# A three-layer fused kernel: the gate's 64-channel chunk in three passes, late weight chunks' low parts on VectorE, six slots' tap sums on TensorE, and a new order

## The chip, the cores and the metric

The kernel runs on one core of one Trainium2 chip. The metric is device microseconds of one execution; of several executions the median is given. The engines are TensorE (PE), VectorE (DVE), ScalarE (ACT), GpSimd (POOL) and SyncE (SP), which here issues every DMA.

## What is computed

Two sequences of 4160 tokens with 192 channels go through three layers, one after another.

```python
# 1: windowed attention, 8 heads, 7 taps
w = exp(weight_gen - max); w = w / (sum(w) + 1e-9)          # over the 7 taps
x = einsum('bshk,bskhg->bshg', w, the last 7 rows of x)
# 2: token-shift mix and a gated square-relu layer, 192 -> 1024 -> 192
xk = mu_k * x + (1 - mu_k) * x_prev                         # x_prev: the row before
xr = mu_r * x + (1 - mu_r) * x_prev
x = sigmoid(xr @ w_r) * (relu(xk @ w_k) ** 2 @ w_v)
# 3: 192 -> 1024 -> 192 with a 3-tap convolution along the sequence
h = relu(x @ w_in)
out = (h * sigmoid(conv3(h, conv_w))) @ w_out
```

The weights arrive in float64, x, weight_gen, `mu_k` and `mu_r` in float32, and the result is float32.

## The kernel before

**Tiles.** The 4160 tokens of a sequence are cut into ten tiles `i`: two of 238 tokens, seven of 476 and one of 352 (`SIZES`). Each is done for both sequences `b`. A partition of the attention stage holds 2, 4 or 3 neighbouring tokens, its slots `l`. The 192 channels are cut into 128 and 64, the 1024 hidden channels into eight chunks `fi`.

**Precision.** A float32 product is made of fp32r passes: a value is split into a high part, which fp32r holds, and a low part, what is left. An ACT cast makes the high part, and a subtract on DVE or POOL the low part. A product against the 192 input channels takes 5 matmul passes (`passes_in`: three of 128 channels, and two in which the 64 remaining channels' high and low inputs lie in the two halves of one 128-lane tile, `xB`). A product from a hidden chunk back to 192 channels takes 5 as well (`out_passes`): `W[:, fi, 2]` has the high part of the 64 remaining output channels in its lower and the low part in its upper 64 columns, and the two halves of the result are added at the end.

**Weights.** Sixteen chunks of weights (`prepare`) are loaded one after another; `narrow` turns float64 bits into float32 in a PSUM bank: an ACT `Prelu`, a shift, a mask and a multiply on DVE, then an identity matmul and a sign matmul on PE. `split` then casts the high part on ACT, subtracts it by a sign matmul on PE, and copies the low part out on ACT. The bank `py` of `narrow` is `pc0`, which later is one of the two banks of the third layer.

**Attention.** For each slot, `token` makes one product of 1344 elements a partition (7 taps x 192) on POOL and then three adds (576, 384 and 192 elements) that sum the taps. In tile 0 alone seven identity matmuls on PE make the sum, and ACT copies it out. The DMA of a tile's rows (`attention.load`) goes into one of two buffers. `softmax` prepares the tap weights; for tiles 3 to 9 its steps run in between, tile by tile.

**Mixing and the layers.** `mixing` transposes tokens to channels on PE, mixes them with the row before (DVE), and splits them, the low parts on POOL; the 64-channel parts go to `xB` by DMA. `gate_r` makes the two chunks of r, `moe1` the eight hidden chunks, `mix_out` multiplies by r and writes the split result to `x2_b`, whose rows 0 and 1 are the 128 channels' high and low part, row 2 the 64 channels' high part (in both halves), and row 3 their high part again in lanes 0 to 63 and their low part in lanes 64 to 127. `moe2` reads it, its fifth pass row 3, and does convolution, sigmoid and `w_out`; `store` adds the two halves and sends the result out.

**Order.** Nothing is issued in the order of the code. Each step is put in a plan at a time (`at`), which the table `ORDER` shifts for single entries by their running number; the plan, in order of time, gives each operation a priority, and `schedule` then issues them by a list schedule with a cost of its own for each kind (`cost`). What comes out is a fixed order on each engine. SP issues DMAs in that order, and a DMA that waits holds all behind it. Line 237, in `schedule`, issues every operation, so all rows of the profile bear it and operations are told apart by their tiles: `pa`, `pc`, `am`, `ar`, `bm` and `br` are PSUM banks (`pa` first products and transposes, `am` and `ar` the second product of layer two, `pc` and `bm`, `br` those of layer three), `prod` and `tok` belong to attention, `xA`, `xB`, `rm` and `mk` to mixing, `s` and `g` are split hidden chunks. `stage` holds weights early on, and softmax sums, `q` and mixing's buffers later.

Of the kernel before, what the change touches and what calls it, by code (L numbers as in the profile page):

```python
# [30 lines left out]
LAG = 12  # L31

# [4 lines left out]
ALONE = 7  # L37
# [55 lines left out]
def f(ap):  # L93
    return ap.bitcast(F32)


class Program:
# [40 lines left out]
    def cost(self, eng, method, out, ins, pointer):  # L138
# [3 lines left out]
        if method == "dma_start":  # L142
            return 0.45, 0.0
# [108 lines left out]
def conv_moe_kernel(ctx: ExitStack, tc: tile.TileContext, xp, wg_first, wg_rest, mus, w_k, w_v, w_r, w_in, conv_w, w_out, out):  # L252
# [35 lines left out]
    mu = new("mu", [128, 4])  # L288
# [22 lines left out]
    wz_r = Ring([t.rearrange("p a b -> p (a b)") for t in g_r.tiles[:2]])  # L311
    rows_r = ring("rows", 2, [128, max(SLOTS) + PAD, DM])
# [16 lines left out]
    sw = new("sw", [128, sum(slots), KS, NH])  # L329
# [67 lines left out]
    on_pe = [False]  # L397

    def narrow(st, n):
# [5 lines left out]
        if on_pe[0]:  # L405

            zr = wz_r()[:, :n]
            ACT.activation(px, f(hi), ACTF.Prelu, scale=2.0 ** -112, alpha=-(2.0 ** 32))
            DVE.tensor_scalar(z, x, 3, None, op0=ALU.logical_shift_left)
            DVE.tensor_scalar(y, z, 0xFF800000, None, op0=ALU.bitwise_and)  # L410
            DVE.scalar_tensor_tensor(out=zr, in0=lo, scalar=2.0 ** -52, in1=py, op0=ALU.mult, op1=ALU.mult)
            PE.matmul(px, lhsT=ident, rhs=f(z), start=True, stop=False, skip_group_check=True)
            PE.matmul(px, lhsT=signs[:, 0:128], rhs=zr, start=False, stop=True, skip_group_check=True)
            return px
        ACT.activation(px, f(hi), ACTF.Copy, scale=2.0 ** -112)
        DVE.tensor_scalar(x, x, 3, None, op0=ALU.logical_shift_left)
        DVE.scalar_tensor_tensor(out=x, in0=hi, scalar=0x80000000, in1=x, op0=ALU.bitwise_and, op1=ALU.bitwise_or)
        DVE.tensor_scalar(y, x, 0xFF800000, None, op0=ALU.bitwise_and)
        DVE.scalar_tensor_tensor(out=f(z), in0=lo, scalar=2.0 ** -52, in1=py, op0=ALU.mult, op1=ALU.mult)
# [58 lines left out]
    def prepare(first, seq):  # L478

        for j, (t, (load, n, go)) in enumerate(seq):  # L480
# [5 lines left out]
            def use(st=st, n=n, go=go, j=j):  # L486
                on_pe[0] = j < 16
                go(narrow(st[0], n))
# [595 lines left out]
```

## Time and profile before

| | |
|---|---|
| median of 3 runs | 736.1 us (734.06, 736.1, 736.75) |
| the profiled execution's own time | 739.15 us |
| its span | 737.3 us |
| mean granted clock of PE | 0.989 of full speed |
| busy: PE, DVE, ACT, POOL | 706.5, 580.1, 646.6, 537.8 us |
| the same, share of the span | 96%, 79%, 88%, 73% |
| share of PE in the chain that ended last | 80%; POOL 8%, ACT 6%, DVE 2%, DMA 1% |

The busy times are averages over very different stages: until some 120 us the weights are prepared and the first, half-size tiles run; then comes a steady stretch; POOL has its attention work until about 515 us and little after that; from 720 us on the last chunks run out. Rows of matmuls overlap, so a row's length is not its price; the pieces of the chain of waits, which follow each other, give that. A bracket at the end of a row of the timeline is the idle time just before it and what ended it. The times of rows are from the start of the span, and the span lies inside the execution's own time, which has 1.85 us more.

### The profile page before, as it was taken

What the parts mean: (1) busy time and instruction counts of PE and PEld (TensorE: products, weight loads), DVE (VectorE), ACT (ScalarE), POOL (GpSimd) and SP (SyncE); (2) the same over time, 40 slices, a digit from 0 to 9 for tenths busy, and PEclk for the clock granted to TensorE, in tenths of its full rate; (3) what the DMA queues carried; (4) which work ended last, traced back from release to release, by engine and by line L of the source; (5) the groups of instructions that cost most, each with busy time, mean ns of one, the idle gap of its engine ahead of it and who ended that gap; (6) DMA issues with size and microseconds to landing.
All of it is one profiled execution on the core that took longest, in us unless ns stands there. A gap on an engine that the chain in (4) does not pass through costs nothing.

```text
span 737.3 us, 10455 instructions
## 1 busy us (share of the span) xinstructions
PE 706.5 (96%) x3475; PEld 607.1 (82%) x3475; DVE 580.1 (79%) x959; ACT 646.6 (88%) x1340; POOL 537.8 (73%) x392
## 2 busy tenths in 40 slices
PE   4899988999999999999999999999999999999996
PEld 4687966888778888888888888888888888899995
DVE  5865968887998988787878787978796758686775
ACT  2788859999989999899989898989899989899986
POOL 1998997898999899999999999999022323242333
PEclk9899999999999999999999999999999999999999
DMA  8667112101211320231112202210002000200000
GB/s 271 196 198 228 56 54 54 39 35 59 68 39 55 88 75 1 73 80 48 54 58 57 87 1 69 74 48 1 21 15 59 1 20 7 55 0 21 1 21 29
DMA packets 18149, 44.58 MB, mean 60 GB/s; under 512 B 2864, under 2 KB 13616, under 8 KB 17968
## 3 DMA queue, kind: packets, MB, share of 16 engines
q1 hardware_dynamic: 18096, 43.93, 19.7%
q8 instruction: 27, 0.44, 0.3%
q14 instruction: 26, 0.21, 0.1%
HBM read 27.40 MB, written 6.39 MB: 46 GB/s over the span
## 4 chain that ended last, share of the span: by engine, by line
PE 80%; POOL 8%; ACT 6%; issue 3%; DVE 2%; DMA 1%; POOLq 0%; SPq 0%; ACTq 0%; DVEq 0%
PE pa L237 25%; PE pc L237 18%; PE bm L237 12%; PE am L237 11%; PE br L237 8%; PE ar L237 7%; POOL prod L237 5%; ACT pa L237 1%; DMA mu<-in_mu_dram 1%; ACT pc L237 1%; POOL s L237 1%; ACT L237 1%; DVE stage L237 1%; POOL xA L237 1%; POOL tok L237 0%
## 5 line engine op out<-in xcount | busy, mean ns | idle before, releaser
L237 DVE SCALAR_TENSOR_TENSOR pc<-h,cw,pc 128x476 f32<-128x476 f32 (+1 forms) x276 | 194.3, 705 | 40.4 <-ACT pc L237 37.4
L237 POOL TENSOR_TENSOR prod<-rows,sw 128x1344 f32<-128x1344 f32 x68 | 210.4, 3096 | 16.1 <-PE pa L237 15.2
L237 ACT ACTIVATE pa<-pa 128x476 f32<-128x476 f32 (+2 forms) x284 | 153.1, 540 | 31.7 <-PE pa L237 28.5
L237 POOL TENSOR_TENSOR prod<-prod 128x576 f32<-128x576 f32 (+1 forms) x132 | 161.5, 1223 | 9.3
L237 PE MATMUL bm<-g,wo 128*128 128x476 f32 (+1 forms) x411 | 133.1, 378 | 3.3 <-ACT g L237 2.8
L237 PE MATMUL am<-s,wv 128*128 128x476 f32 (+2 forms) x464 | 135.1, 359 | 0.0
L237 PE MATMUL pa<-xA,wkA 128*128 128x476 f32 (+2 forms) x450 | 117.6, 366 | 2.0 <-DVE s L237 1.5
L237 POOL TENSOR_TENSOR g<-stage,g 128x476 fp32r<-128x476 f32 (+1 forms) x41 | 47.5, 1158 | 97.5 <-ACT g L237 93.6
L237 PE MATMUL pc<-x,wiA 128*128 128x478 f32 (+1 forms) x414 | 113.2, 379 | 0.7 <-ACT x L237 0.6
L237 PE MATMUL ar<-s,wv 128*128 128x476 f32 (+2 forms) x336 | 106.5, 355 | 3.6 <-ACT s L237 3.6
L237 DVE TENSOR_TENSOR s<-pa,s 128x476 fp32r<-128x476 f32 (+1 forms) x139 | 88.1, 634 | 18.7 <-ACT s L237 18.2
L237 PE MATMUL br<-g,wo 128*128 128x476 f32 (+1 forms) x274 | 102.5, 375 | 0.0
L237 PEld LDWEIGHTS pa<-xA,wkA 128*128 128x128 f32 x450 | 79.7, 189 | 19.1 <-DVE s L237 5.5
L237 ACT ACTIVATE pc<-h,cw 128x476 f32<-128x476 f32 (+1 forms) x138 | 92.4, 670 | 1.2
L237 PEld LDWEIGHTS am<-s,wv 128*128 128x128 f32 x464 | 82.1, 189 | 11.2 <-ACT s L237 0.9
L237 DVE TENSOR_TENSOR pc<-h,pc 128x476 f32<-128x476 f32 x96 | 62.8, 654 | 33.7 <-ACT pc L237 33.5
L237 PEld LDWEIGHTS bm<-g,wo 128*128 128x128 f32 x411 | 75.9, 188 | 15.4 <-ACT g L237 4.3
L237 ACT ACTIVATE pc<-pc 128x476 f32<-128x476 f32 (+1 forms) x148 | 81.2, 548 | 8.2 <-DVE pc L237 6.5
L237 PEld LDWEIGHTS pc<-x,wiA 128*128 128x128 f32 x414 | 76.2, 190 | 12.7 <-DVE g L237 2.0
L237 ACT ACTIVATE h<-pc 128x478 f32<-128x478 f32 (+1 forms) x138 | 79.0, 573 | 8.4 <-PE pc L237 7.5
L237 PE MATMUL pa<-xB,wkB 128*128 128x476 f32 (+2 forms) x300 | 84.5, 361 | 0.6 <-DMA xB<-mk 0.6
L237 PE MATMUL pc<-x,wiB 128*128 128x478 f32 (+1 forms) x276 | 82.4, 377 | 0.0
(161 smaller groups left out, 1190.0 us busy)
## 6 DMA issues: line engine op xcount, KB each, us to landing
rows<-in_x_dram SPq DMA_DIRECT2D x14, 960.0 KB, 4.8
xB<-rm SPq DMA_DIRECT2D x28, 119.0 KB, 2.3
rows<-in_x_dram SPq DMA_DIRECT2D x4, 768.0 KB, 6.5
xB<-mk SPq DMA_DIRECT2D x16, 119.0 KB, 2.3
rows<-in_x_dram SPq DMA_DIRECT2D x2, 864.0 KB, 4.3
out_dram<-stage SPq DMA_DIRECT2D x7, 238.0 KB, 2.0
out_dram<-om SPq DMA_DIRECT2D x7, 238.0 KB, 2.0
stage<-in_moe_w_v_dram SPq DMA_DIRECT2D x4, 384.0 KB, 6.0
```

The source lines that it names most:

```text
L237: getattr(self.real[eng], method)(*a, **k)
```

## The change

1. *Gate.* In `gate_r` the chunk `k` = 1, 64 channels, takes 3 passes instead of 5: columns 128 to 191 of `w_r`'s high part and, at columns 192 to 255, its low part, which two DMAs (`swap`) put there, stand side by side in one stationary matrix. `fold` then adds the result's upper 64 lanes to its lower ones (an ACT copy and a DVE add), the sigmoid runs on 64 lanes, and an SP DMA copies r to the other 64. Tiles 2 to 9 use it, 16 times.
2. *Late weight chunks.* By `MODES`, chunks 8, 9, 10 and 12 to 15 (`w_in` and `w_out`; 11 is the convolution's) no longer use identity and sign matmuls: `narrow` leaves three parts, and `split` takes the low part from them by a subtract and an add on DVE. `pc0` is held until the last add.
3. *Tap sums.* For the six slots of `SUMS`, of tiles 1 and 2, PE sums the taps, as in tile 0, and ACT copies the sum; POOL makes the product alone.
4. *mu* stands in the first load's tensor; its own DMA is gone.
5. *mix_out.* The high part in row 3 of `x2_b` is copied from row 2 by an SP DMA instead of an ACT copy.
6. *Softmax of tiles 3 to 9.* z + 1e-9 is done by ACT instead of DVE; its load has another time.
7. *The last tile's second sequence.* POOL, not ACT, casts the high parts of `g` for chunks 0 to 4; DVE, not POOL, subtracts for chunks 6 and 7; the last chunk's two closing passes change places.
8. *Order.* The table `ORDER` is another one throughout, with entries for plan numbers up to 2999.

```diff
+HIGH = range(5)
+LOWS = {(NTILE - 1, NB - 1, k) for k in range(6, NF)}
+SUMS = {(1, 1, 0), (1, 1, 1), (2, 0, 2), (2, 0, 3), (2, 1, 2), (2, 1, 3)}
+MODES = [0, 0, 0, 0, 0, 0, 0, 0, 2, 2, 2, 0, 2, 2, 2, 2, 2]
 ORDER = {
-    11: 0.0501, 14: 1.7001, 15: 1.6002, 29: -0.0009, 53: 1.9991, 66: -0.0803, 69: -1.0999, 70: -0.6499, 71: -0.6499,
...
+    3: -0.7006000000000228, 4: -5.900400000000019, 5: -6.000200000000007, 6: -6.100100000000012,
...
@@ cost @@
-            return 0.45, 0.0
+            return 0.58 if src == ["SBUF"] else 0.45, 0.0
@@ narrow @@
+        ACT.activation(px, f(hi), ACTF.Prelu, scale=2.0 ** -112, alpha=-(2.0 ** 32))
...
         DVE.tensor_scalar(x, x, 3, None, op0=ALU.logical_shift_left)
-        DVE.scalar_tensor_tensor(out=x, in0=hi, scalar=0x80000000, in1=x, op0=ALU.bitwise_and, op1=ALU.bitwise_or)
         DVE.tensor_scalar(y, x, 0xFF800000, None, op0=ALU.bitwise_and)
-        DVE.scalar_tensor_tensor(out=f(z), in0=lo, scalar=2.0 ** -52, in1=py, op0=ALU.mult, op1=ALU.mult)
-        DVE.tensor_tensor(px, px, f(z), op=ALU.add)
-        return px
+        zr = wz_r()[:, :n] if mode[0] == 1 else py
+        DVE.scalar_tensor_tensor(out=zr, in0=lo, scalar=2.0 ** -52, in1=py, op0=ALU.mult, op1=ALU.mult)
+        return Parts(px, wl_r()[:, :n], zr)
@@ split @@
+        if isinstance(x, Parts):
+            px, zl, zr = x.aps
+            ACT.copy(dst_hi, px)
...
+                DVE.tensor_tensor(zl, px, f(dst_hi), op=ALU.subtract)
+                DVE.tensor_tensor(dst_lo, zr, f(zl), op=ALU.add)
+            return
@@ softmax @@
         def s5():
-            DVE.tensor_scalar(z, z, 1e-9, None, op0=ALU.add)
+            if bank is None:
+                ACT.activation(z, z, ACTF.Copy, bias=1e-9)
+            else:
+                DVE.tensor_scalar(z, z, 1e-9, None, op0=ALU.add)
@@ attention @@
-            if i < 1:
+            if i < 1 or (i, b, l) in SUMS:
...
+                    if i:
+                        ACT.copy(x[:, l], z)
+                        return
@@ gate_r @@
-            sl = slice(128 * k, 128 * k + 128)
-            mm(p[:, :N], passes_in(wrA, wrB, xin[i, b, 1, 0], xin[i, b, 1, 1], sl, N))
+            A, B = xin[i, b, 1, 0], xin[i, b, 1, 1]
+            if k:
+                mm(p[:, :N], [(wrA[:, 0, 128:256], A[:, 0, :N]), (wrA[:, 0, 128:256], A[:, 1, :N]), (wrB[:, 0, 128:256], B[:, :N])])
+            else:
+                mm(p[:, :N], passes_in(wrA, wrB, A, B, slice(0, 128), N))
+        def fold():
+            a = attt_r()[0:64, :N]
+            ACT.copy(a, st["p"][64:128, :N])
+            DVE.tensor_tensor(st["p"][0:64, :N], st["p"][0:64, :N], a, op=ALU.add)
...
-            ACT.activation(r[:, :N], st["p"][:, :N], ACTF.Sigmoid)
+            ACT.activation(r[h, :N], st["p"][h, :N], ACTF.Sigmoid)
+            if k:
+                SP.dma_start(out=r[64:128, :N], in_=r[0:64, :N])
@@ out_passes @@
-        PE.matmul(am[:, :n], lhsT=W[:, fi, 0], rhs=s1, start=False, stop=z, skip_group_check=one)
-        PE.matmul(ar[:, :n], lhsT=W[:, fi, 2], rhs=s1, start=False, stop=z, skip_group_check=one)
+        for p, k in ((ar, 2), (am, 0)) if back else ((am, 0), (ar, 2)):
+            PE.matmul(p[:, :n], lhsT=W[:, fi, k], rhs=s1, start=False, stop=z, skip_group_check=one)
@@ mix_out @@
-            ACT.copy(X[0:64, 3, c], r[0:64, :N])
             ACT.copy(X[:, 2, c], r[:, :N])
+            SP.dma_start(out=f(X[0:64, 3, c]), in_=f(X[0:64, 2, c]))
@@ moe2 @@
-            ACT.copy(g[:, 0, :N], st["q"][:, :N])
+            if (i, b) == (NTILE - 1, NB - 1) and fi in HIGH:
+                POOL.tensor_copy(g[:, 0, :N], st["q"][:, :N])
+            else:
+                ACT.copy(g[:, 0, :N], st["q"][:, :N])
...
-            (POOL if i >= ALONE else DVE).tensor_tensor(g[:, 1, :N], st["q"][:, :N], f(g[:, 0, :N]), op=ALU.subtract)
+            (POOL if i >= ALONE and (i, b, fi) not in LOWS else DVE).tensor_tensor(g[:, 1, :N], st["q"][:, :N], f(g[:, 0, :N]), op=ALU.subtract)
@@ the plan @@
-    softmax_load(3, wg_rest[:, (slots[1] + slots[2]) * KH:], 18.2, 50.0)
+    softmax_load(3, wg_rest[:, (slots[1] + slots[2]) * KH:], 20.5, 60.0)
+    def swap():
+        for W in (wrA, wrB):
+            SP.dma_start(out=f(W[:, 0, DM:256]), in_=f(W[:, 1, 128:DM]))
+    at(30.5, swap)
```

Three places of the order follow. A number behind a name's underscore counts the kernel's tiles, and one before it is the ring's place.

POOL, at the tokens of tile 2. Before (`rows0` is sequence 0's rows, `rows1` sequence 1's; the adds of a slot follow its product):

```order
L237 TENSOR_TENSOR prod1_84<-rows0_81,sw_112 128x1344
L237 TENSOR_TENSOR prod1_84<-prod1_84 128x576
L237 TENSOR_TENSOR prod1_84<-prod1_84 128x384
L237 TENSOR_TENSOR tok0_85<-prod1_84 128x192
L237 TENSOR_TENSOR prod0_83<-rows1_82,sw_112 128x1344
L237 TENSOR_TENSOR prod0_83<-prod0_83 128x576
L237 TENSOR_TENSOR prod0_83<-prod0_83 128x384
L237 TENSOR_TENSOR tok0_85<-prod0_83 128x192
L237 TENSOR_TENSOR prod1_84<-rows1_82,sw_112 128x1344
L237 TENSOR_TENSOR prod1_84<-prod1_84 128x576
L237 TENSOR_TENSOR prod1_84<-prod1_84 128x384
L237 TENSOR_TENSOR tok0_85<-prod1_84 128x192
```

After:

```order
L645 TENSOR_TENSOR prod0_82<-rows0_80,sw_111 128x1344
L645 TENSOR_TENSOR prod1_83<-rows0_80,sw_111 128x1344
L645 TENSOR_TENSOR xA01_93<-mk0_88,xA01_93 128x238
L645 TENSOR_TENSOR xA11_95<-mk1_89,xA11_95 128x238
L645 TENSOR_TENSOR prod0_82<-rows1_81,sw_111 128x1344
L645 TENSOR_TENSOR prod0_82<-prod0_82 128x576
L645 TENSOR_TENSOR prod0_82<-prod0_82 128x384
L645 TENSOR_TENSOR tok0_84<-prod0_82 128x192
L645 TENSOR_TENSOR prod0_82<-rows1_81,sw_111 128x1344
L645 TENSOR_TENSOR prod1_83<-rows1_81,sw_111 128x1344
L645 TENSOR_TENSOR prod1_83<-prod1_83 128x576
L645 TENSOR_TENSOR prod1_83<-prod1_83 128x384
```

Two products of sequence 0 now stand back to back with no adds behind them, tile 1's `xA` low parts come after them, and of the two products of sequence 1 shown one has its adds and one has not.

DVE, at a late chunk of 512 columns of `w_in`. Before (`bm` is the bank that the chunk is narrowed in, `g0` takes the product that goes to the sign matmul):

```order
L237 TENSOR_SCALAR stage_76<-bm_119 128x512
L237 TENSOR_SCALAR stage_76<-br_120 128x384
L237 TENSOR_SCALAR pc0_115<-stage_76 128x512
L237 SCALAR_TENSOR_TENSOR mk0_89<-pc1_116,mu_61,att0_87 128x238
L237 SCALAR_TENSOR_TENSOR g0_77<-stage_76,pc0_115 128x512
L237 TENSOR_TENSOR s3_108<-pa1_114,s3_108 128x476
L237 TENSOR_SCALAR pc0_115<-stage_76 128x384
L237 SCALAR_TENSOR_TENSOR mk1_90<-pc1_116,mu_61,att1_88 128x238
L237 SCALAR_TENSOR_TENSOR g1_78<-stage_76,pc0_115 128x384
```

After (`wiA` is the weights' tile):

```order
L645 TENSOR_SCALAR bm_118<-bm_118 128x512
L645 TENSOR_SCALAR pc0_114<-bm_118 128x512
L645 SCALAR_TENSOR_TENSOR pc0_114<-stage_75,pc0_114 128x512
L645 TENSOR_TENSOR g3_79<-bm_118,wiA_67 128x512
L645 TENSOR_TENSOR s2_106<-pa1_113,s2_106 128x476
L645 TENSOR_TENSOR wiA_67<-pc0_114,g3_79 128x512
L645 TENSOR_TENSOR s3_107<-pa0_112,s3_107 128x476
```

The shift, the mask and the multiply stand as before, now in the banks themselves; a subtract into `g3` and an add that writes the low part to `wiA` are added, with a low part of a hidden chunk (`s2`) between them.

SP, at the loads of tile 5's rows and the second layer's results. Before:

```order
L237 DMA out_0_dram<-om0_111 128x475
L237 DMA out_0_dram<-stage_76 64x475
L237 DMA rows0_81<-in_x_dram 128x1920
L237 DMA out_0_dram<-stage_76 128x476
L237 DMA out_0_dram<-att1_88 64x476
L237 DMA rows1_82<-in_x_dram 128x1920
L237 DMA xB02_99<-rm00_91 64x476
L237 DMA xB00_97<-rm00_91 64x476
L237 DMA xB12_102<-rm10_92 64x476
```

After (`r10` is the gate's second chunk, `x2_0` and `x2_1` what the third layer reads):

```order
L645 DMA out_0_dram<-om0_110 128x475
L645 DMA out_0_dram<-att1_87 64x475
L645 DMA x2_1_74<-x2_1_74 64x476
L645 DMA rows0_80<-in_x_dram 128x1920
L645 DMA r10_103<-r10_103 64x476
L645 DMA out_0_dram<-stage_75 128x476
L645 DMA out_0_dram<-att1_87 64x476
L645 DMA rows1_81<-in_x_dram 128x1920
L645 DMA x2_0_73<-x2_0_73 64x476
```

The copies of r and of the third layer's input stand between stores and row loads; the last one shown is right behind a load of rows.

## Rows read from the trace of the kernel before

**Rows 1.** Windows: stretch, length, busy PE, PEld, DVE, ACT, POOL, PEclk, DMA, GB/s

```profile
60.00:117.00 57.00, 49.50 (x319) 42.58 (x318) 43.48 (x72) 43.03 (x96) 51.15 (x38) 0.97 0.32 103
117.00:210.00 93.00, 91.15 (x419) 76.97 (x420) 79.87 (x132) 87.30 (x172) 85.02 (x60) 0.98 0.16 46
720.00:733.00 13.00, 11.16 (x55) 8.57 (x55) 8.86 (x18) 9.97 (x24) 6.58 (x7) 1.00 0.07 21
```

**Rows 2.** Chain of waits, its pieces on PE: start, length, what, instructions

```profile
146.78 1.08 PE pc L237 x5
17.10 0.86 PE bm L237 x2
22.84 0.23 PE bm L237
23.31 2.29 PE pa L237 x14
```

**Rows 3.** Groups by form, POOL: count, then busy us, mean ns, idle before

```profile
L237 POOL TENSOR_TENSOR prod<-rows,sw 128x1344 f32<-128x1344 f32 x68 | 210.4, 3096 | 16.1 <-PE pa L237 15.2 <-PE pc L237 0.4
L237 POOL TENSOR_TENSOR prod<-prod 128x576 f32<-128x576 f32 x66 | 94.4, 1431 | 4.4
L237 POOL TENSOR_TENSOR prod<-prod 128x384 f32<-128x384 f32 x66 | 67.0, 1016 | 4.9
L237 POOL TENSOR_TENSOR tok<-prod 128x192 f32<-128x192 f32 x66 | 39.5, 599 | 4.8
```

**Rows 4.** Chain of waits, 62 to 118 us: first and last of POOL's pieces

```profile
62.85 1.43 POOL prod L237
113.47 1.23 POOL mk L237
```

**Rows 5.** Timeline of PE: start, length, operation, idle before and releaser

```profile
117.01 0.67 PE L237 MATMUL pa<-xB,wkB 128*128 128x476 f32 x2 [0.60 <-DMA xB<-mk]
119.09 0.60 PE L237 MATMUL ar<-s,wv 128*128 128x238 f32 x3 [1.41 <-ACT s L237]
219.43 0.93 PE L237 MATMUL pa<-xA,wkA 128*128 128x476 f32 x3 [1.35 <-DVE s L237]
```

**Rows 6.** Windows around two gaps of PE (columns as in the first group)

```profile
92.70:94.70 2.00, 0.03 (x1) 0.00 (x0) 1.11 (x2) 2.00 (x6) 2.00 (x1) 1.00 0.00 0
96.30:99.80 3.50, 3.50 (x15) 3.17 (x14) 1.59 (x3) 1.41 (x3) 3.34 (x4) 0.51 0.00 0
120.30:123.80 3.50, 3.50 (x14) 3.17 (x13) 1.42 (x3) 2.64 (x6) 3.42 (x2) 0.51 0.00 0
```

**Rows 7.** Timeline of DVE: onemu, and two steps of softmax

```profile
8.43 0.17 DVE L237 TENSOR_SCALAR onemu<-mu 128x4 f32<-128x4 f32 x1 [2.58 <-DMA mu<-in_mu_dram]
205.69 0.19 DVE L237 TENSOR_SCALAR stage<-stage 128x64 f32<-128x64 f32 x1
216.14 2.06 DVE L237 TENSOR_SCALAR stage<-stage 128x48 f32<-128x48 f32 x1
```

**Rows 8.** Groups by form, DVE, ACT and POOL (columns as for POOL)

```profile
L237 DVE TENSOR_TENSOR s<-pa,s 128x476 fp32r<-128x476 f32 x123 | 79.8, 649 | 16.2 <-ACT s L237 15.9
L237 ACT CAST x<-ar 64x476 fp32r<-64x476 f32 x14 | 7.9, 563 | 0.0
L237 POOL TENSOR_TENSOR s<-stage,s 128x354 fp32r<-128x354 f32 x7 | 6.6, 950 | 6.5 <-ACT s L237 6.5
```

**Rows 9.** Timelines of ACT and PE around one mix_out, and a DMA issue row

```profile
351.79 0.58 ACT L237 CAST x<-ar 128x476 fp32r<-128x476 f32 x1
360.69 0.60 PE L237 MATMUL pc<-x,wiB 128*128 128x478 f32 x2
xB<-rm SPq DMA_DIRECT2D x28, 119.0 KB, 2.3
```

**Rows 10.** Timelines of POOL and ACT at the end

```profile
731.31 0.94 POOL L237 TENSOR_TENSOR s<-stage,s 128x354 fp32r<-128x354 f32 x1 [0.67 <-ACT s L237]
732.77 0.46 ACT L237 COPY om<-bm 128x353 f32<-128x353 f32 x1 [1.54 <-PE bm L237]
```

More of the change, by code (lines that the diff above doesn't have):

```diff
@@ L251, in conv_moe_kernel @@
 @with_exitstack
-def conv_moe_kernel(ctx: ExitStack, tc: tile.TileContext, xp, wg_first, wg_rest, mus, w_k, w_v, w_r, w_in, conv_w, w_out, out):
+def conv_moe_kernel(ctx: ExitStack, tc: tile.TileContext, xp, wg_first, wg_rest, w_k, w_v, w_r, w_in, conv_w, w_out, out):
     nc = tc.nc
@@ L285, in __call__ @@
             return self.tiles[(self.n - 1) % len(self.tiles)]
-    mu = new("mu", [128, 4])
     onemu = new("onemu", [128, 4])
@@ L311, in conv_moe_kernel @@
     wz_r = Ring([t.rearrange("p a b -> p (a b)") for t in g_r.tiles[:2]])
+    wl_r = Ring([t.rearrange("p a b -> p (a b)") for t in g_r.tiles[2:]])
     rows_r = ring("rows", 2, [128, max(SLOTS) + PAD, DM])
@@ L328, in conv_moe_kernel @@
     KH = KS * NH
-    sw = new("sw", [128, sum(slots), KS, NH])
+    both = new("sw", [128, 4 + sum(slots) * KH])
+    mu = both[:, 0:4]
+    sw = both[:, 4:].rearrange("p (s k h) -> p s k h", k=KS, h=NH)
     sm = []
@@ L395, in fetch, with __init__, rearrange, __getitem__ @@
         return st
-    on_pe = [False]
+    mode = [0]
+    class Parts:
+        def __init__(self, *aps):
+            self.aps = aps
+        def rearrange(self, *a, **k):
+            return Parts(*(x.rearrange(*a, **k) for x in self.aps))
+        def __getitem__(self, c):
+            return Parts(*(x[c] for x in self.aps))
     def narrow(st, n):
@@ L404, in narrow @@
         x, y, z = px.bitcast(U32), py.bitcast(U32), wy_r()[:, :n]
-        if on_pe[0]:
+        ACT.activation(px, f(hi), ACTF.Prelu, scale=2.0 ** -112, alpha=-(2.0 ** 32))
+        if mode[0] == 0:
             zr = wz_r()[:, :n]
-            ACT.activation(px, f(hi), ACTF.Prelu, scale=2.0 ** -112, alpha=-(2.0 ** 32))
             DVE.tensor_scalar(z, x, 3, None, op0=ALU.logical_shift_left)
@@ L414, in narrow @@
             return px
-        ACT.activation(px, f(hi), ACTF.Copy, scale=2.0 ** -112)
         DVE.tensor_scalar(x, x, 3, None, op0=ALU.logical_shift_left)
-        DVE.scalar_tensor_tensor(out=x, in0=hi, scalar=0x80000000, in1=x, op0=ALU.bitwise_and, op1=ALU.bitwise_or)
         DVE.tensor_scalar(y, x, 0xFF800000, None, op0=ALU.bitwise_and)
-        DVE.scalar_tensor_tensor(out=f(z), in0=lo, scalar=2.0 ** -52, in1=py, op0=ALU.mult, op1=ALU.mult)
-        DVE.tensor_tensor(px, px, f(z), op=ALU.add)
-        return px
+        zr = wz_r()[:, :n] if mode[0] == 1 else py
+        DVE.scalar_tensor_tensor(out=zr, in0=lo, scalar=2.0 ** -52, in1=py, op0=ALU.mult, op1=ALU.mult)
+        return Parts(px, wl_r()[:, :n], zr)
     def split(dst_hi, dst_lo, x):
+        if isinstance(x, Parts):
+            px, zl, zr = x.aps
+            ACT.copy(dst_hi, px)
+            if mode[0] == 1:
+                DVE.tensor_tensor(zl, px, f(dst_hi), op=ALU.subtract)
+                PE.matmul(px, lhsT=signs[:, 0:128], rhs=zl, start=True, stop=False, skip_group_check=True)
+                PE.matmul(px, lhsT=signs[:, 0:128], rhs=zr, start=False, stop=True, skip_group_check=True)
+                ACT.copy(dst_lo, px)
+            else:
+                DVE.tensor_tensor(zl, px, f(dst_hi), op=ALU.subtract)
+                DVE.tensor_tensor(dst_lo, zr, f(zl), op=ALU.add)
+            return
         ACT.copy(dst_hi, x)
-        if on_pe[0] and prog.space(x) == "PSUM":
+        if prog.space(x) == "PSUM":
             PE.matmul(x, lhsT=signs[:, 128:256], rhs=dst_hi, start=False, stop=True, skip_group_check=True)
@@ L486, in use @@
             def use(st=st, n=n, go=go, j=j):
-                on_pe[0] = j < 16
+                mode[0] = MODES[j]
                 go(narrow(st[0], n))
@@ L495, in softmax_load @@
     def softmax_load(j, wg, t, hold=0.0):
-        w = sm[j][0]
-        at(t, lambda: SP.dma_start(out=w.rearrange("p s k h -> p (s k h)"), in_=wg), hold)
+        w = both[:, (4 + KH * soft_at[j]) * (j > 0):4 + KH * soft_at[j + 1]]
+        at(t, lambda: SP.dma_start(out=w, in_=wg), hold)
     def softmax(j, a, b, eng, times, bank):
@@ L676, in sg @@
             r_t[k] = r
-            ACT.activation(r[:, :N], st["p"][:, :N], ACTF.Sigmoid)
+            ACT.activation(r[h, :N], st["p"][h, :N], ACTF.Sigmoid)
+            if k:
+                SP.dma_start(out=r[64:128, :N], in_=r[0:64, :N])
+        h = slice(0, 64 if k else 128)
         at(t, go)
-        at(t + 0.3, sg)
+        if k:
+            at(t + 0.2, fold)
+        at(t + (0.6 if k else 0.3), sg)
     def moe1(i, b, fi, t):
@@ L795, in mix_out_half, with out_passes @@
         at(t + 0.4, d2)
-    def out_passes(W, fi, s, n, am, ar, one=False):
+    def out_passes(W, fi, s, n, am, ar, one=False, back=False):
         s0, s1 = s[:, 0, :n], s[:, 1, :n]
@@ L889, in c7 @@
             st["g"] = g
-            ACT.copy(g[:, 0, :N], st["q"][:, :N])
+            if (i, b) == (NTILE - 1, NB - 1) and fi in HIGH:
+                POOL.tensor_copy(g[:, 0, :N], st["q"][:, :N])
+            else:
+                ACT.copy(g[:, 0, :N], st["q"][:, :N])
         def c8():
             g = st["g"]
-            (POOL if i >= ALONE else DVE).tensor_tensor(g[:, 1, :N], st["q"][:, :N], f(g[:, 0, :N]), op=ALU.subtract)
+            (POOL if i >= ALONE and (i, b, fi) not in LOWS else DVE).tensor_tensor(g[:, 1, :N], st["q"][:, :N], f(g[:, 0, :N]), op=ALU.subtract)
         def go2():
@@ L899, in go2 @@
                 acc2["r"] = br_r()
-            out_passes(wo, fi, st["g"], N, acc2["m"], acc2["r"])
+            out_passes(wo, fi, st["g"], N, acc2["m"], acc2["r"], back=last and b == NB - 1 and fi == NF - 1)
         at(t + 0.5, go)
@@ L940, in consts @@
     def consts():
-        SP.dma_start(out=mu, in_=mus)
         DVE.tensor_scalar(onemu, mu, -1.0, 1.0, op0=ALU.mult, op1=ALU.add)
@@ L1020, in conv_moe_kernel @@
         prog.schedule()
-_ARGS = ("x", "first", "rest", "mu", "moe_w_k", "moe_w_v", "moe_w_r", "moe2_w_in", "moe2_conv_w", "moe2_w_out")
+_ARGS = ("x", "first", "rest", "moe_w_k", "moe_w_v", "moe_w_r", "moe2_w_in", "moe2_conv_w", "moe2_w_out")
 def _layout(inputs):
@@ L1048, in _layout @@
     w = np.asarray(inputs["weight_gen"]).transpose(0, 1, 3, 2)
+    mu = np.stack([c for k in "kr" for m in [rows(inputs["moe_mu_" + k]).reshape(DM)]
+                   for c in (m[:128], np.concatenate([m[128:], m[128:]]))], axis=1)
     a = {
         "x": np.concatenate([np.zeros_like(x[:, :PAD]), x], axis=1),
-        "first": chunks(w, 0, 1),
+        "first": np.concatenate([mu, chunks(w, 0, 1)], axis=1),
         "rest": chunks(w, 1, NTILE),
-        "mu": np.stack([c for k in "kr" for m in [rows(inputs["moe_mu_" + k]).reshape(DM)]
-                        for c in (m[:128], np.concatenate([m[128:], m[128:]]))], axis=1),
         "moe_w_k": rows(inputs["moe_w_k"]),
```

500 rows, old and new, of the table ORDER are left out of this document.

## The prediction

> **What bounds the kernel now.** I read the busy shares first, then the windows, then the chain of waits, then single rows. TensorE (PE) is busy for 96% of the span and nearly the whole chain of the second half runs on it, so the span is PE's work plus PE's gaps: a change must take work off PE or close a gap. In the steady stretch from 117 to 210 us PE is busy 91.15 of 93.00 us, ScalarE (ACT) 87.30, GpSimd (POOL) 85.02 and VectorE (DVE) 79.87 [rows 1]: little is to be had there but PE's own work. From 60 to 117 us PE is busy only 49.50 of 57.00 us at a granted clock of 0.97, and POOL 51.15 us. The gap there is 7.5 us, and the missing 0.03 of the clock over 49.5 us is another 1.5 us: **9.0 us lost** in one stretch. The chain names the cause: from 62.85 to 113.47 us it is 31 pieces of POOL with nothing between them but issue time and POOL's queue, products and tap sums for the tokens of tiles 1 and 2 above all, and the last is the low part of tile 2's mixed input [rows 4]. Behind it PE still waits 1.41 us for ACT just ahead of 119.09 us [rows 5], and after the two gaps come two stretches of 3.50 us at half clock, 96.30 to 99.80 and 120.30 to 123.80 us, 0.51 of full, the 1.2 GHz level; in front of the first PE had stood for 2.00 us with 0.03 us of work [rows 6]. Later there is one more stall of 1.35 us ahead of 219.43 us [rows 5], and the tail, where 11.16 of 13.00 us are busy [rows 1].
>
> **PE's work.** A pass of 476 columns is 1.08 / 5 = 0.216 us [rows 2]; one of 352 I estimate as 0.216 x 352 / 476 = 0.16. *Gate:* the 64-channel chunk goes from 5 passes to 3 for 14 gates of 476 columns and 2 of 352: 28 x 0.216 + 4 x 0.16 = 6.7 us less. *Late weight chunks:* a 512-column chunk loses the two identity matmuls (0.86 us) and two sign matmuls (0.23 us each) [rows 2], 1.32 us; one of 384 columns 0.75 of that, 0.99. Three and four of them: 8.0 us less. *Tap sums:* a slot's sum on PE is 14 instructions in 2.29 us [rows 2], six of them 13.7 us more. Net **-1.0 us**. So PE pays the gate's and the chunks' savings to POOL; what counts is when POOL is done.
>
> **POOL's release, the largest term.** A slot's three adds are 1.431 + 1.016 + 0.599 = 3.05 us [rows 3]; six slots, all in tiles 1 and 2, take 18.3 us off POOL ahead of tile 2's mixing, and the order shows tile 2's POOL rows closing up accordingly. That is twice the 9.0 us that PE loses in this stretch, so POOL stops being the last to arrive and PE's own work sets the stretch. I take all of the 9.0 us: **-9.0**. What is late next is PE itself, ACT's six copies of a sum (128x192 each, under 0.6 us apiece by the 64x476 copy of 0.563 us [rows 8]) and DVE (first rival). The stall at 119.09 us and the half-clock stretch behind it, 1.41 + 3.5 x 0.49 = 3.1 us, come of the same late arrival, but ACT ends that wait, not POOL; between 0 and 3.1 us I take the middle, **-1.5**.
>
> The Trainium skill, "TensorE: Matmul & The Clock Gate", Part 1, says that the default state of the clock is throttled and that activity releases it. The rows agree: a gap of 2.00 us, then 3.50 us at 0.51 [rows 6]. By that rule the second term is not a middle: it is all (-3.1) if no gap opens there, or nothing; the sum below would be 1.6 lower or 1.5 higher.
>
> **The stall at 219 us.** DVE's z + 1e-9 takes 0.19 us at 205.69 us, but 2.06 us at 216.14 us [rows 7], where POOL's 3.096 us product [rows 3] runs; a hidden softmax step thus stretches, DVE's following low part is late, and PE stalls 1.35 us. Moving the add to ACT takes this row off DVE; ACT pays seven short steps of 64 columns, beside PE's work. **-1.35.** This is the only one of these rows that PE waits for; the others are hidden.
>
> **The tail.** POOL's subtract of 0.94 us at 731.31 us ends the last wait of PE, and then the copies of `om` (0.46 us) and `att` follow each other on ACT [rows 10]. DVE does a 128x476 subtract in 0.649 us [rows 8], so 0.649 x 354 / 476 = 0.48 for 354 columns: 0.46 less on the path. Finishing `br` a pass early lets the `att` copy start first: up to 0.46 less. Casts on POOL for chunks 0 to 4 free ACT, but each puts work on POOL ahead of its own subtract of 0.950 us [rows 8]; between -0.6 (13.00 - 11.16 = 1.84 us of gaps, a third closed) and +1.8 (they double) I take -0.3, because ACT and POOL alternate here and either may be late. Sum **-1.2**, ends -1.5 and +1.0.
>
> Here a rule speaks against the change. The row shows a one-operand DVE instruction stretched by POOL's traffic [rows 7]. The Trainium skill, "GPSIMD Engine Reference", section 1, says that GpSimd shares its SBUF interfaces with VectorE, with contention for DVE instructions in a 2-port perf mode or with two SBUF inputs. The subtracts that go to DVE read two SBUF tiles, so by the page each may wait for a POOL step; with up to 0.95 us each the tail would be +0.7 instead of -1.2 and the sum 1.9 higher. No row of before shows that pair.
>
> **The start.** `onemu` waits 2.58 us for mu on DVE and the first product follows at 8.51 us [rows 7]; the product also needs its rows, so the one small load less is worth at most 0.3, I take **-0.2**. Its cover, the rows load, stays.
>
> **What is added beside PE.** *DVE:* each late chunk gets a subtract and an add, by the 0.649 us of 476 columns [rows 8] 0.70 each for 512 and 0.52 for 384: 3 x 1.40 + 4 x 1.04 = 8.4 us; the 16 folds 14 x 0.649 + 2 x 0.48 = 10.0 us; the z adds go, seven rows between 0.19 and 2.06 us, Net about +15 us on an engine with 13 us free in each 93 [rows 1]: hidden when spread over the span, tight only where the chunks lie. *ACT:* 16 fold copies in (0.563 us each by the 64x476 row), 16 X copies of the same shape out [rows 8]: nil; the chunks' low casts leave. *SyncE (SP):* 16 copies of r, 16 of X, two swaps, one load less: 33 more DMAs. Each such transfer lands 2.3 us after issue [rows 9]. In before X's row 3 is written by ACT by 352.4 us and read by PE's wiB pass at 360.69 us [rows 9]: 8.3 us of slack, less 2.3 for landing and an allowance of 0.5 for the issue leaves 5.5 us for SP's queue. So I cost these DMAs at nothing; their cover is that slack. The swap stands among tile 2's xB copies and waits for the last gate of tile 1; behind it are four xB copies that PE needs for its first tile-2 pass. POOL's tokens come at least as late, so nothing is added. The fold lengthens the gate's own chain by an ACT and a DVE step (0.56 + 0.65 us), but r is not wanted until the eighth chunk of the same layer has been multiplied.
>
> **The sum.** Against the profiled execution: -1.0 - 9.0 - 1.5 - 1.35 - 1.2 - 0.2 = -14.25 us. Its span of 737.3 becomes 723.05, with the 1.85 us outside the span 724.9 us. That execution (739.15 us) lay 3.05 us above the median of 736.1, so the median comes to **722 us**. The ends of the terms give 720 (-3.1 for -1.5, -1.5 for the tail) and 729 (two thirds of the 9.0, nothing for the -1.5, +1.0 for the tail).
>
> **Rivals.**
> *DVE becomes the early bound: 728 us.* In 60 to 117 us DVE is busy 43.48 us [rows 1]. With the chunks' 8.4 us that is 51.9 us of work, and after my gain the stretch has 48: by this 3.9 us of the 9.0 don't come, nor the 1.5 behind them, and DVE holds bank pc0, which moe2 needs, until the last add. 722 + 5.4 = 727.4, with the fold of a gate in it 728. Against it: the new order has fewer tile-2 low parts ahead of this place, so not all of the 43.48 stays there.
> *The gate's saving doesn't arrive: 728.7 us.* The change does what it says, but the passes saved become waits, because ACT (87.30 of 93.00 [rows 1]) is as full as PE. 722 + 6.7. Against: ACT's sum of added and removed work is near nil or below, and ACT would have only 6.7 us less room in some 600.
> *Slower: X's row 3 waits in SP's queue: 742 us.* SP issues in order. At three places of the new order (tile 3 for both sequences, tile 5 for the first) the copy of X's third row stands right behind a load of rows, and that load waits until POOL has read the buffer's old content. A slot on POOL is 3.096 + 3.05 = 6.15 us [rows 3]. If POOL is two slots (12.3 us) later than the order assumes, each copy is 12.3 - 5.5 = 6.8 us late for PE: 3 x 6.8 = 20.4, 742 us. It decides from a lateness of 5.5 us on; it makes the kernel slower than now from about 10.3 us. Against: POOL has 18.3 us less to do just there.
>
> **How the numbers follow.** Forecast 722 (its own range 717 to 729, the ends above and below them the 2.7 us by which the runs of before differ): 0.62. DVE as the early bound: 0.19. Gate saving lost: 0.07. SP's queue: 0.07. The rest, 0.05, is a gain beyond my sum: the gaps left between 117 and 210 us and in the tail (1.85 + 1.84 us, part of them counted) closed, and more. What this kernel's measurement can tell from no change is about 0.5%, 3.7 us, so faster means under 732.4 us and slower over 739.8. Forecast, gain beyond it and both middle rivals lie on the faster side (0.93); for terms that fail together I move 0.07 of it to "same". Range 712 to 732: it takes in the forecast, both middle rivals and most of the better case, and leaves out SP's queue.
>
> **What would show it.** Right: in the changed kernel the 60 to 117 us window has PE busy by over 54 us a window of 57, no POOL chain of tens of pieces ahead of tile 2, and the first tile-2 passes start some 10 us earlier than 117.01 us [rows 5]; PE's busy total falls by about 1 us only; no half-clock window around 96 or 120 us; no PE stall near 219 us; the end of PE to the end of the span shorter by about half a microsecond. Wrong: PE waiting for DVE in rows of pc or bm between 60 and 110 us (first rival); PE waiting for ACT or DVE throughout (second); PE's moe2 wiB passes waiting for a DMA of x2 (third).

## The result, and the profile after

The changed kernel takes **714.93 us** (median of 4 runs, 714.17 to 716.51) against 736.15 us (four runs) before: the ratio is 0.9719, with a 95% interval of 0.9693 to 0.9746, 21.2 us less. The profiled execution took 715.5 us, its span is 713.6 us and its granted clock 1.0. The forecast was 722 us with a range of 712 to 732: the sign and the range held, but the sum was 14 us where 21 came.

Two lines of the page, busy time by engine and the chain that ended last:

```profile
PE 696.0 (98%) x3495; PEld 603.2 (85%) x3495; DVE 588.3 (82%) x992; ACT 635.4 (89%) x1337; POOL 519.7 (73%) x377
PE 72%; ACT 4%; DVE 2%; issue 1%; POOL 0%; POOLq 0%
```

POOL, 8% of the chain before, is gone from it. The windows, with the columns of [rows 1]:

```profile
60.00:107.00 47.00, 45.13 (x322) 42.67 (x321) 41.11 (x74) 38.73 (x84) 45.18 (x29) 1.00 0.36 119
60.00:117.00 57.00, 55.13 (x368) 51.03 (x367) 50.49 (x89) 48.10 (x104) 54.51 (x34) 1.00 0.30 98
117.00:210.00 93.00, 92.78 (x429) 77.51 (x428) 81.70 (x133) 88.15 (x179) 79.09 (x57) 1.00 0.20 60
210.00:220.00 10.00, 10.00 (x48) 8.51 (x47) 8.71 (x16) 9.61 (x20) 9.69 (x7) 1.00 0.06 15
```

From 60 to 117 us PE is busy 55.13 us at full clock, where it was 49.50 us at 0.97 [rows 1], and there is no gap at all from 210 to 220 us. Nor has the stall of 219 us only moved earlier: from 117 to 210 us PE lacks 0.22 us in all. The first pass of tile 2 on `xB` starts at 101.01 us, not 117.01 [rows 5], and the longest wait of PE in this stretch is one of 1.40 us for ACT's copy of a tap sum:

```profile
92.04 0.55 PE L645 MATMUL pa<-ident,tok 128*128 128x128 f32 x3 [1.40 <-ACT tok L645]
101.01 0.59 PE L645 MATMUL pa<-xB,wkB 128*128 128x476 f32 x2
```

Two of the signs that the prediction named as right did not come. PE's busy total fell by 10.5 us (706.5 to 696.0) and not by about 1. And the span ends some 4.4 us behind PE's last matmul in both kernels, where half a microsecond less was expected.

### The profile page after: what moved, and what is told of

Its sections match the earlier page's. It is cut to its first block, busy times and chain, and to the rows that moved or that the text cites. A ratio compares the mean times of both kernels' runs of the same rounds, so it can differ in the third digit from the quotient of the medians.

```text
span 713.6 us, 10565 instructions
## 1 busy us (share of the span) xinstructions
PE 696.0 (98%) x3495; PEld 603.2 (85%) x3495; DVE 588.3 (82%) x992; ACT 635.4 (89%) x1337; POOL 519.7 (73%) x377
## 4 chain that ended last, share of the span: by engine, by line
PE 72%; ACT 4%; DVE 2%; issue 1%; POOL 0%; POOLq 0%
PE pa L645 21%; PE pc L645 17%; PE bm L645 10%; PE am L645 10%; PE br L645 7%; PE ar L645 7%; ACT pc L645 1%; DVE pc L645 1%; DVE stage L645 1%; ACT pa L645 1%; ACT h L645 0%; POOL s L645 0%; ACT L645 0%; ACT stage L645 0%; DVE pa L645 0%
## 5 line engine op out<-in xcount | busy, mean ns | idle before, releaser
L645 POOL TENSOR_TENSOR prod<-rows,sw 128x1344 f32<-128x1344 f32 x68 | 210.2, 3094 | 17.6 <-PE pa L645 13.7
L645 DVE SCALAR_TENSOR_TENSOR pc<-h,cw,pc 128x476 f32<-128x476 f32 (+1 forms) x270 | 190.9, 708 | 26.9 <-ACT pc L645 24.1
L645 ACT ACTIVATE pa<-pa 128x476 f32<-128x476 f32 (+2 forms) x290 | 156.4, 545 | 12.0 <-PE pa L645 10.2
L645 POOL TENSOR_TENSOR prod<-prod 128x576 f32<-128x576 f32 x120 | 147.0, 1225 | 8.1
L645 DVE TENSOR_TENSOR s<-pa,s 128x476 fp32r<-128x476 f32 (+1 forms) x142 | 89.7, 635 | 26.1 <-ACT s L645 25.4
L645 PEld LDWEIGHTS pa<-xA,wkA 128*128 128x128 f32 x468 | 81.5, 188 | 14.0 <-DVE s L645 2.0
L645 ACT ACTIVATE pc<-h,cw 128x476 f32<-128x476 f32 (+1 forms) x135 | 90.3, 669 | 0.8
L645 ACT ACTIVATE pc<-pc 128x476 f32<-128x476 f32 (+1 forms) x142 | 78.6, 554 | 12.6 <-DVE pc L645 10.2
L645 ACT ACTIVATE h<-pc 128x478 f32<-128x478 f32 (+1 forms) x135 | 77.3, 573 | 13.2 <-PE pc L645 12.2
L645 PEld LDWEIGHTS pc<-x,wiA 128*128 128x128 f32 x414 | 73.8, 188 | 16.1 <-DVE g L645 4.7
L645 ACT CAST s<-pa 128x476 fp32r<-128x476 f32 (+1 forms) x142 | 78.9, 561 | 1.0
```

Source lines behind the costliest of these rows:

```text
L645: getattr(self.real[eng], method)(*a, **k)
```

## The experiments

Parts were undone one at a time in the changed kernel. Since the planner would lay out every engine's queue anew for any edit, the runs whose names begin with f_ keep its plan: the order is worked out from the changed kernel's operations, and the part's instructions are put in place of others only when they are issued. Times are compared with the changed kernel's 714.93 us or, where it is named, the kernel before.

**The kernel before once more.**

> The kernel before itself, for a second profile. If the late mu (2.58 us of DVE's waiting) belongs to every execution, its row stands here again, with the first product near 8.5 us; if it was that one execution, which took 739.15 us, the product starts near 6 us. The half-clock stretches: if they belong to the order, they stand at the same places (near 32 to 38, 96 to 100 and 120 to 124 us); if they are chance, elsewhere or not at all.

It took 736.05 us, the median. DVE's rows at the start, and the windows around its three half-clock stretches:

```profile
5.92 0.17 DVE L237 TENSOR_SCALAR onemu<-mu 128x4 f32<-128x4 f32 x1
6.00 3.02 DVE L237 TENSOR_TENSOR prod<-rows,sw 128x1344 f32<-128x1344 f32 x2
28.00:35.00 7.00, 6.60 (x20) 4.77 (x21) 6.51 (x14) 4.85 (x15) 6.76 (x6) 0.51 0.87 282
92.00:97.00 5.00, 4.83 (x24) 4.47 (x24) 2.60 (x5) 2.11 (x5) 4.76 (x5) 0.66 0.01 2
116.00:121.00 5.00, 4.83 (x19) 4.23 (x20) 2.50 (x5) 3.85 (x8) 4.83 (x3) 0.66 0.14 31
```

DVE does not wait for mu here; the 2.58 us of [rows 7] belonged to the one execution that was profiled first, which lay 3.05 us above the median. The half-clock stretches stand at the same three places of the program, some 3 us earlier. They cost 7.00 x 0.49 + 5.00 x 0.34 + 5.00 x 0.34 = 6.8 us. That does not make them certain. b_mu, the run told next, has the same order on PE and the same gap at the second place (1.99 us of idle time, in b_again ahead of 91.43 us), but no half-clock stretch behind it:

```profile
92.27 0.60 PE L237 MATMUL ar<-s,wv 128*128 128x238 f32 x3 [1.99 <-ACT s L237]
92.00:97.00 5.00, 4.56 (x29) 4.13 (x30) 3.63 (x7) 3.63 (x8) 4.76 (x4) 1.00 0.00 2
```

So the place makes such a stretch likely, and chance has a part in it. Of 19 executions of the kernel before, three had a mean granted clock of 0.993 and took 733.4 to 734.8 us; the others, at 0.988 to 0.991, took 735.5 to 738.2 us. In the changed kernel the window in the first place reads 1.00:

```profile
28.00:35.00 7.00, 6.59 (x37) 4.59 (x36) 6.50 (x13) 6.94 (x20) 6.69 (x7) 1.00 0.91 308
```

PE is busy for as long, 6.59 us, but gets 37 matmuls done instead of 20 (not all of the same kind). No trace of the changed kernel, or of its variants f_modes0, f_gate5, f_x3, f_z, a_tail and a_mu, has a half-clock stretch while PE works. The span of this execution is 734.3 us, 20.7 above the changed kernel's; a third of that is the clock.

**mu in the first load, alone and taken out.**

```diff
 # b_mu, in the kernel before
-    mu = new("mu", [128, 4])
-        SP.dma_start(out=mu, in_=mus)
+    both = new("sw", [128, 4 + sum(slots) * KH])
+    mu = both[:, 0:4]
 # a_mu, in the changed kernel
+        SP.dma_start(out=mu, in_=mus)
```

> The kernel before with mu in the first load alone; the order on PE, ACT and POOL is unchanged. If mu's own transfer held DVE (as the bracket of its onemu row said), the first product starts near 5.9 us instead of 8.51 and everything follows 2.6 us earlier: 733.5 us; some 3 us less again, 730.5 us, if the half-clock stretch at 31.8 to 38.2 us goes with it. If the rows' load is the limit, as my prediction had it, the product starts after 8.2 us and the time is 735.8 to 736.1 us.

> The changed kernel with mu in a DMA of its own again, as SP's fourth, and onemu on DVE just ahead of the first product; the order on PE, ACT and POOL is unchanged. If mu's transfer holds the first product and the changed kernel keeps what it wins at the start, 2.6 us more: 717 to 718 us. If, as in the kernel before with mu in the first load (735.81 against 735.95 us), a later start is made good further on, or mu lands in time in most executions: 714 to 715.8 us.

Alone it gives 735.81 us (ratio 1.0007, 0.9988 to 1.0025), and taken out it costs 715.67 - 714.93 = 0.7 us, inside the spread of either kernel. This part is worth nothing that can be measured.

**Tap sums back on POOL.**

```diff
 # f_nosums: at the place of the product
+    POOL.tensor_tensor(y[:, 0:3], y[:, 0:3], y[:, 3:6], op=ALU.add)
+    POOL.tensor_tensor(y[:, 0:2], y[:, 0:2], y[:, 2:7:4], op=ALU.add)
+    POOL.tensor_tensor(dst, y[:, 0], y[:, 1], op=ALU.add)
-    PE.matmul(z, lhsT=ident, rhs=y[:, k], ...)     # 7 for each of 6 slots
-    ACT.copy(x[:, l], z)
```

> The changed kernel, every other operation in the same place, but the six slots' tap sums back on POOL (three adds right behind the product), PE's 42 matmuls gone. Theory POOL's release: POOL is 18.3 us later ahead of tile 2, PE waits there again, and although it has 13.7 us less to do the time rises to between 722 and 733 us, with a gap and half-clock stretches between 85 and 120 us. Rival, PE or DVE sets the early pace: PE's 13.7 us come off and the time is 701 to 715 us.

728.1 us, 13.2 more, although PE has by the prediction's estimate 13.7 us less to do. Its window and its longest wait there:

```profile
60.00:117.00 57.00, 42.01 (x273) 39.03 (x273) 41.09 (x74) 37.82 (x80) 55.20 (x40) 0.85 0.28 96
101.18 0.90 PE L651 MATMUL pa<-ident,tok 128*128 128x128 f32 x3 [7.69 <-POOL tok L995]
```

PE stands idle for 15 of 57 us, 7.69 of them in one wait for POOL's last add (L995 is that add), and half clock is back (0.85 in the mean). POOL's release is shown, and so is its second effect: the gap itself is not all that it costs. The 13.2 us are what undoing costs in a plan that was made for the sums on PE; a plan of its own might save some of it.

**Late weight chunks back on PE.**

```diff
 # f_modes0 and f_modes0b
-    DVE.tensor_tensor(zl, px, f(dst_hi), op=ALU.subtract)
-    DVE.tensor_tensor(dst_lo, zr, f(zl), op=ALU.add)
+    PE.matmul(px, lhsT=ident, rhs=f(z), ...); PE.matmul(px, lhsT=signs[:, 0:128], rhs=w, ...)
+    PE.matmul(px, lhsT=signs[:, 128:256], rhs=dst_hi, ...); ACT.copy(dst_lo, px)
```

> The changed kernel, every other operation in the same place, but the seven late weight chunks narrowed and split as before (identity and sign matmuls on PE, low part copied by ACT). Theory PE is the bound early: 8.0 us more PE work, 722 to 724 us. Rival, DVE is the early bound in the changed kernel: its 8.4 us less pay for it, 713 to 717 us.

> As f_modes0, but the sign matmul and both casts of a late chunk stand behind the identity matmul (there the cast could come ahead of it). PE's 8.0 us more and what waits come with it: 722 to 726 us if PE is the bound early, under 717 us if DVE is.

In the first of the two the cast to the high part could come ahead of the identity matmul and read an unfinished sum, so it computes with other weights; its instructions are the same in number. It took 725.08 us, 10.2 more and a little above what was expected: 8.0 us of PE's work by the prediction's estimate, which leaves some 2 us for waits. In the second, with the steps in a right order, PE's queue meets the sign matmuls too soon for ACT, and it took 734.36 us, far above the expected 722 to 726:

```profile
50.45 0.79 PE L871 MATMUL bm<-x,signs 128*128 128x512 f32 x1 [5.09 <-ACT x L870]
40.00:60.00 20.00, 14.52 (x86) 12.62 (x86) 7.40 (x14) 10.16 (x23) 9.76 (x6) 0.91 0.56 147
```

One wait of 5.09 us, and half clock behind it. How much of the 19.4 us a plan made for this variant would save is open. Both tell against DVE as the early bound: DVE has its 8.4 us back, is busy for only 7.40 of 20 us here, and the kernel is slower each time.

**The gate in five passes.**

```diff
 # f_gate5
-    mm(p[:, :N], [(wrA[:, 0, 128:256], A[:, 0, :N]), (wrA[:, 0, 128:256], A[:, 1, :N]), (wrB[:, 0, 128:256], B[:, :N])])
+    mm(p[:, :N], passes_in(wrA, wrB, A, B, slice(128, 256), N))
```

> The changed kernel, every other operation in the same place, but the gate's 64-channel chunk in 5 passes with no fold, no copy of r and no swap. Theory PE-bound: 6.7 us more PE work, 721 to 722 us. Rival, the saved passes had become waits for ACT or DVE: 713 to 717 us.

720.04 us, 5.1 more. Most of the 6.7 us of passes arrives; that the fold and the copies take the other 1.6 us is likely, but they were not tried apart.

**z on DVE, and X's third row by ACT.**

```diff
 # f_z
-                ACT.activation(z, z, ACTF.Copy, bias=1e-9)
+                DVE.tensor_scalar(z, z, 1e-9, None, op0=ALU.add)
 # f_x3
-            SP.dma_start(out=f(X[0:64, 3, c]), in_=f(X[0:64, 2, c]))
+            ACT.copy(X[0:64, 3, c], r[0:64, :N])
```

> The changed kernel, every other operation in the same place, but softmax's z + 1e-9 on DVE again. Theory, a DVE step is stretched beside POOL's product and PE waits for what DVE has behind it, in one of seven places: 716 to 717 us, and a row of over 1 us among these steps. Rival, no place is so tight: 714 to 715.5 us.

> The changed kernel, every other operation in the same place, but the high part of the 64 channels in the third row copied by ACT again, 14 x 0.56 us and two shorter ones, and 16 DMAs fewer. If ACT has the room, as I costed it at nothing: 714 to 716 us. If ACT is next to PE in being full, its 8.8 us show in part: 717 to 722 us. If the DMAs wait in SP's queue in the changed kernel, it becomes faster: under 713.5 us.

f_z: 715.03 us, nothing. Its rows, and POOL's next to them:

```profile
165.82 0.21 DVE L954 TENSOR_SCALAR stage<-stage 128x64 f32<-128x64 f32 x1
166.48 0.52 DVE L954 TENSOR_SCALAR stage<-stage 128x64 f32<-128x64 f32 x4
169.81 1.15 POOL L651 TENSOR_TENSOR sw<-sw,stage 128x448 f32<-128x448 f32 x1 [5.57 <-DVE stage L651]
```

The new order puts five of the seven steps where POOL is idle for 5.57 us, and they last about 0.22 us each (four in a row, which overlap, take 0.52 us together). The longest of all seven lasts 0.51 us. The stall went by the order, not by the move to ACT.

f_x3: 718.36 us, 3.4 more. Its chain that ended last:

```profile
PE 65%; ACT 10%; DVE 3%; issue 1%; DVEq 0%
```

ACT has 10% of the chain where the changed kernel has 4%. No single wait tells it: the longest of PE's between 130 and 690 us is 0.2 us. PE's 3495 matmuls are the same in number, but count as busy for 698.4 us, 2.4 more; so most of the time seems lost in waits too short to show as gaps. ACT is the engine that is full next to PE, and 8.8 us taken off it count for 3.4. Whether ACT's load does it or the place is not shown: in f_x3, as in the kernel before, the copy stands on ACT ahead of that of row 2, which the third layer needs as well.

**The tail.**

```diff
 # a_tail
-HIGH = range(5)
-LOWS = {(NTILE - 1, NB - 1, k) for k in range(6, NF)}
+HIGH, LOWS = (), set()
 # and the two closing passes in the old order
```

> The changed kernel with the last sequence's casts back on ACT, its last two subtracts back on POOL, and the two closing passes in the old order; elsewhere the order is nearly unchanged (18 places on PE). My prediction's tail term gives +1.2 us, 716.1 us; by the two profiles, in which the stretch behind the last full tile shrank by 3.2 us, it is 717.5 to 718.5 us.

716.98 us, 2.05 more in the medians. The size is uncertain: the four times (715.87 to 717.32) overlap with the changed kernel's (714.17 to 716.51), and the spans of the two profiled executions, 714.1 and 713.6 us, differ by 0.5 us. Rows of POOL and PE near its end, and of DVE and ACT in the changed kernel:

```profile
707.93 0.94 POOL L645 TENSOR_TENSOR s<-stage,s 128x354 fp32r<-128x354 f32 x1 [0.65 <-ACT s L645]
708.92 0.43 PE L645 MATMUL bm<-s,wo 128*128 128x354 f32 x1 [0.27 <-POOL s L645]
```

```profile
707.18 1.17 DVE L645 TENSOR_TENSOR s<-stage,s 128x354 fp32r<-128x354 f32 x2
709.03 0.45 ACT L645 COPY stage<-br 64x353 f32<-64x353 f32 x1 [1.24 <-PE br L645]
```

With the change PE waits for no low part at the end (0.27 us in a_tail, with the POOL step of 0.94 us in front), and the copy of `br`, which has another step behind it, goes ahead of the copy of `om` at 709.51 us. The three parts were not tried one by one.

**Both kernels without their tables.**

```diff
 # a_noorder, b_noorder
-ORDER = {...}
+ORDER = {}
```

> The changed kernel with its table of shifts empty, so that the planner orders everything by the code's own times. With the next run it tells parts from order. If the parts (gate, chunks, sums, mu, tail) are the gain, this kernel is some 15 to 25 us faster than the kernel before without its table. If the new order is the gain, the two are within 8 us of each other.

> The kernel before with its table of shifts empty. The old table's worth is what this is above 736 us: 5 to 20 us by the many places at which PE's gaps are small in the kernel before.

728.22 us for the changed kernel (ratio to the kernel before 0.9884, 0.9855 to 0.9912) and 738.71 us for the kernel before (1.0040, 1.0022 to 1.0058). Without tables the parts are worth 10.5 us (two runs of the one, eight of the other). The old table was worth 2.6 us, less than the 5 to 20 expected, the new one 13.3. Neither of the two answers that I had set out is right: it is half and half. Which of the new table's shifts bring the 13.3 us was not tried, nor the new order without the parts. Without its table the changed kernel has gaps and half-clock stretches again:

```profile
60.00:117.00 57.00, 49.76 (x315) 45.17 (x314) 43.54 (x81) 40.51 (x86) 48.39 (x34) 0.94 0.31 106
28.00:33.00 5.00, 4.01 (x14) 3.06 (x15) 4.65 (x11) 3.81 (x12) 4.76 (x5) 0.66 0.98 294
```

## Why the prediction was right, and where its steps were off

*What bounds the kernel.* Right. PE's work and PE's gaps make the span, and POOL made the gaps between 60 and 117 us for the most part: with its adds put back PE is idle for 15 us there (f_nosums).

*PE's work, -1.0.* Right in its parts as far as they were tried: the gate's passes arrive nearly whole (5.1 of 6.7 us), the chunks cost at least their 8.0 us when put back (10.2), and the sums' 13.7 us were well paid for. Its sign, a busy total lower by about 1 us, was wrong, for the most part because PE also counts as busy while its clock is halved; see the sum.

*POOL's release, -9.0.* Right in mechanism and near in size. In the window from 60 us to 107, 10 us shorter as forecast, PE loses 47.00 - 45.13 = 1.9 us instead of 9.0: 7.1 us of the 9.0 came. One reading was too simple. The chain's last POOL piece, at 113.47 us, had waited 3.72 us for an ACT step (`rm`), which the chain shows as issue time; so POOL's own work did not fill the whole chain.

*The stall at 119 us and its half clock, -1.5.* Mis-sized, and this is the largest miss. I had weighed the clock as a by-product of two gaps: 1.5 us within the 9.0, and 0.9, half of 1.7, in this term. Both profiles of the kernel before have 6.8 us in three stretches, the first of which (28 to 35 us in the second profile) no step of mine priced at all, and all of them are gone. That is some 4.4 us more than counted. The Trainium skill, "TensorE: Matmul & The Clock Gate", Part 1, says that activity releases the throttle. Read as all or nothing it would have given the right side of the choice here, since every stretch went whole: 0.51, 0.66 and 0.66 in the kernel before, 1.00 in the changed one, 0.85 where POOL's adds are put back. But b_mu has a gap of 1.99 us with no stretch behind it, so that a gap costs its stretch each time is not shown.

*The stall at 219 us, -1.35.* The stall went, and its cause was read rightly, but not what removed it. The step of 2.06 us (48 columns, the last of the seven) ends at 218.20 us, where POOL's product beside it ends at 218.15. I costed the move to another engine where the place in the order was what mattered: back on DVE, in the new order, it costs nothing (f_z).

*The tail, -1.2.* Right in sign, as far as the medians tell; the size is open, 2.05 us in the medians and 0.5 in the two profiles. The step that failed is the copy of `br`: finishing it first was to bring the end of the span nearer to PE's end, which stays at some 4.4 us. PE's last wait for a low part did go. The Trainium skill, "GPSIMD Engine Reference", section 1, names contention with GpSimd for DVE instructions with two SBUF inputs. The two DVE subtracts are of that kind, but POOL is done before they start, and they took 1.17 us together; no run here shows that pair.

*The start, -0.2.* The size was right, with the wrong row behind it: I argued that the product needs its rows anyway, while in the profiled execution mu really was last. What made the part worthless is that mu was in time, or late by about a microsecond, in the other executions seen.

*What is added beside PE, at nothing.* Wrong for one of them. I set 16 ACT copies that come against 16 that go and called it nil; but the two kinds were separate choices, and the X copies alone, moved to SP, are worth 3.4 us (f_x3), most likely since ACT is nearly as full as PE. SP's queue carried them without harm. DVE's busy time rose by 8.2 us (580.1 to 588.3) instead of about 15.

*The rivals.* DVE as the early bound fell by f_modes0 and f_modes0b, the lost gate saving by f_gate5, SP's queue by f_x3, which is slower and not faster without the copies of X.

*The sum.* The two profiles, 734.3 us (b_again) and 713.6 us, tell where the 20.7 us between them lie. PE's idle time fell from 28.4 to 17.6 us, by 10.8; the gaps in my sum come to nearly the same, 10.9 (7.5 + 0.7 + 1.35 + 1.2 + 0.2). PE's busy time fell from 705.9 to 696.0 us, by 9.9, of which 6.8 are the clock, where I had 2.4, and 3.1 are left for work and for waits too short to show as gaps (f_x3 adds 2.4 us of busy time of that kind), where I had 1.0. So the gaps came out right in the sum, the clock is 4.4 us short and the rest 2.1. Within the gaps the terms do not hold singly (POOL's release 1.9 us less than forecast, others more), and that their sum fits so well is partly luck. The undone parts give no better account, since in a plan made for all of them they need not add up: sums, chunks and gate alone come to 28.5 us when undone one by one. What I left out as a term is the order itself. I took it as given and read from it only what moved; by the two runs without tables half of the gain needs the new table.

## What to carry to other kernels

Where a gap of TensorE is followed by a stretch at half clock, price the two together, as a likely cost and not a certain one, and look for such stretches over the whole span, not only at the gap in question. Work on an engine that is nearly as full as the bounding one is not free: price what leaves it and what comes to it one by one. A stall of microseconds that is seen in one profiled execution, which lies above the median, wants a second profile before it carries a term.

## What the runs showed of the hardware

Two executions of one kernel had their half-clock stretches at the same three places of the program (0.51 of full behind a gap of 1.99 us, for one). A third, with the same order on PE and the same gap, had no stretch there. So they belong to the work in front of them, but not every execution pays for each.

A DVE step that adds a constant, in place, to 48 columns took 2.06 us beside POOL's product [rows 7] and 0.18 us in f_z. Of these steps in the first profile of the kernel before, four met a POOL instruction with over half a microsecond left, and each ended 0.04 to 0.06 us behind it: at 218.20 us against 218.15, 213.40 against 213.36, 187.46 against 187.40 and 117.58 against 117.52. The second profile has the same four, 0.04 to 0.06 us behind. So such a step lasted as long as the rest of POOL's instruction, whatever its own work; with POOL idle, steps of 64 columns took about 0.22 us (f_z).
